# A conditioned state-space and gated-MLP block: column values in PSUM, the skip term's diagonal built on the chip, and a new order for the side jobs

## The chip, the cores and the metric

The kernel runs on one core of one Trainium2 chip. Its time is the device time in microseconds of one execution. Beside it stands one execution taken with the hardware profiler, from which the engines' instructions, their waits and the DMA transfers are read. Engines are named as the profile names them: PE (TensorE matmul), PEld (TensorE weight load), DVE (VectorE), ACT (ScalarE), POOL (GpSimd), SP (SyncE, which only starts transfers here).

## The reference

One sequence of 2048 rows and 640 channels goes through a layer with adaptive layer norms. All is float32.

```python
mod = (silu(c) @ w_mod).reshape(1, 6, 1, 640)          # sa, ca, ga, sb, cb, gb
h = layernorm(x) * (1 + ca) + sa
# state-space convolution, 192 complex modes for each of the 640 channels d
K[d, l] = Re(sum_n C[d, n] * exp(dt[d] * A[d, n] * l) * dt[d] * B[d, n])   # l = 0..2047
y = irfft(rfft(h, 4096) * rfft(K, 4096))[:2048] + h * Dskip
x = x + ga * y
h = layernorm(x) * (1 + cb) + sb
x = x + gb * (((h @ w_gate) * (h @ w_up)) @ w_down)    # 640 -> 1536 -> 640
```

## The kernel before

The 640 channels are five blocks db = 0..4 of 128. For each block the kernel of the convolution, K, is never exponentiated position by position. From **seeds** (a few powers for each mode) it builds tables of phases and of magnitudes, and takes products of matrices of them.

The program has four stretches. Up to about 26 us the seeds of block 0 are made. Then come 40 **steps** n = 0..39, eight for each block, each of 16 channels; step n is three thirds t = 3n, 3n+1, 3n+2. In a step POOL builds the phase table Ph (integers, so that a turn wraps by itself) and the magnitude tables EQ and EP as outer products (L817, `outer`); ACT takes absolute value and sine and cosine of Ph (its helper is L320, to which every ACT operation is put down; tiles tra and trb hold the result); DVE multiplies the two into QtA, PtA, PtB and QtB (L872, L878, L898); PE multiplies P by Q into the PSUM tile kg (L913 for the A half, kg_ma, and L928 for the B half, kg_mb). Every second step a kg tile is complete and goes through ACT into Kt and from there into the forward transform by matrices (L950, L974, L995), the product with the transformed input (L1036 to L1042, on DVE) and the inverse transform (L1055, L1110). Phase table Ph(n), EQ(n) and EP(n) each have two buffers; QtA, QtB and PtB have one, so DVE's QtA(n+1) waits for PE's kg_ma(n).

All other work is cut into **side jobs** that are slipped in between the thirds:

- w_mod is loaded a third at a time into t_tw and t_ti (1600 KB each, L451), which hold constants of the transform later; PE multiplies it by silu(c) into rows of PSUM (L458), and ACT copies the rows out (TVa, TVb).
- u_fold (L470 to L505) turns the three rows of the first half into columns (PE, L477), works out the gain and shift columns from them on DVE (L481 to L492) and spreads the shift over partitions (PE, L498, L499). The layer norm's gain is folded into the channel's scale dt2 and into the skip column dcol.
- the 16 tiles of x are loaded (`<-A_u`, L560), and DVE takes their statistics (L568); rstd (L371 to L378, called by row_stats for tiles 0 to 5 and then 6 to 15) turns them into 1/sigma and -mean/sigma; ACT normalises and the tiles are stored to DRAM as hm (L580).
- the seeds of blocks 1 to 4, in 14 segments each (L642 to L760, with parts on every engine), the second half of block 0's magnitude seeds (`e0`: ACT's exponentials of LP, RH and RL between two table loads), and the phase and magnitude seeds' doubling on POOL (L777, `tab_ph` and `tab_eq`).

A table of numbers, SCHED, sets where each job stands. A number v belongs to slot v // 1000: slots -101 to -86 lie in the set-up, slots 0 to 241 are the two calls due(2t) and due(2t+1) of each third t, and 287 is the last step; the remainder orders jobs within a slot. A second table, SLOT, gives for each ring of buffers (PSUM's three banks psfa, psfb, psfc, and TV, W, f16, gh, hf and others in SBUF) the letter that each request in turn takes.

The **skip term** h * Dskip enters K at l = 0. The tile dskt [128 x 160] is zero but for one row in each quarter of partitions, filled by transfers: four 1x8x4 pieces of Dskip for block 0 in the set-up (L1410); for the other blocks, whose Dskip is scaled by the gain, dcol goes to DRAM (dgd, L492) and comes back in four 1x32x4 pieces (L508, dskip). Every second step a matmul of 8 columns adds it to kg (L917).

After the steps the rest of the transform runs to 485 us, and then the gated MLP to the end, with matrices in high and low halves (L1160 splits them, L1196 and L1611 are the products).

## Time and profile before

| what | value |
|---|---|
| three runs | 995.63, 998.5, 999.91 us, median 998.5 |
| the profiled execution's own time | 990.33 us |
| its span | 988.6 us |
| its mean granted clock of TensorE | 0.958 |
| PE, DVE, ACT, POOL busy | 90%, 77%, 59%, 58% of the span |
| matmuls, DVE, ACT, POOL instructions | 11190, 1311, 1019, 424 |
| w_mod pieces, issue to landing | 7.4 us and 7.5 us (medians) |

A row of the timeline or of a group gives the start, the time that the engine was busy (for xN, N instructions together), engine, line, operation, output and inputs, shapes and, in brackets, how long the engine stood idle before it and what it waited for last. A row of windows gives, for one stretch of time, each engine's busy time and its instructions, the granted clock (PEclk, 1.00 is full) and the transfers' share.

### The profile page before, as it was taken

Reading aid. Unit: us, or ns where it says so; the run is one execution under the profiler, and the core shown is the slowest. Engines: PE = TensorE matmul, PEld = TensorE weight load, DVE = VectorE, ACT = ScalarE, POOL = GpSimd, SP = SyncE. Lnnn points to the kernel's source line nnn. Section 1 sums busy time; section 2 is a strip of 40 time slices with the busy share of each in tenths; the row PEclk is TensorE's granted clock in tenths of the full one; section 3 lists DMA queues with packets and bytes.
Section 4 is the critical chain, followed back from the end, with each engine's and each line's share of the span. In section 5 each row is a group of like instructions: output and inputs, shape, how many; then the busy total and the mean of one; then the engine's idle time right before and its main releaser. Section 6 shows DMA issues by size and latency. Waiting matters only on the chain.

```text
span 988.6 us, 26668 instructions
## 1 busy us (share of the span) xinstructions
PE 887.3 (90%) x11190; PEld 726.3 (73%) x11190; DVE 760.7 (77%) x1311; ACT 579.9 (59%) x1019; POOL 577.4 (58%) x424
## 2 busy tenths in 40 slices
PE   4854898999798699989988999999999999999998
PEld 3643656676575477677666888889998888889998
DVE  8798479887988977896899877787585977677452
ACT  5769999977888797974664322235464332224330
POOL 4987899799779989960145667641022454451000
PEclk9976899999989989999999999999999999999999
DMA  7665666443545553558733453445536222212241
GB/s 243 240 172 196 224 211 205 142 138 120 142 151 142 172 155 106 183 187 281 217 102 106 134 186 104 137 159 168 198 134 216 85 80 80 81 54 77 83 161 54
DMA packets 141961, 148.96 MB, mean 151 GB/s; under 512 B 8976, under 2 KB 120080, under 8 KB 140432
## 3 DMA queue, kind: packets, MB, share of 16 engines
q1 hardware_dynamic: 140688, 146.33, 46.9%
q8 instruction: 88, 1.44, 0.6%
q10 hardware_dynamic: 1152, 0.92, 0.3%
q14 instruction: 33, 0.27, 0.1%
HBM read 108.36 MB, written 38.86 MB: 149 GB/s over the span
## 4 chain that ended last, share of the span: by engine, by line
PE 58%; DVE 14%; ACT 13%; issue 6%; POOL 5%; DMA 2%; SPq 0%; DVEq 0%; ACTq 0%; POOLq 0%
PE pa L1196 26%; PE pa L1611 16%; ACT tra L320 2%; ACT trb L320 2%; PE psfb L995 2%; DVE QtA L872 2%; PE psfc L995 2%; PE psfb L1055 1%; PE kg L928 1%; POOL EQ L817 1%; PE psfa L1055 1%; PE kg L913 1%; PE psfc L1055 1%; PE psfb L950 1%; PE psfa L995 1%
## 5 line engine op out<-in xcount | busy, mean ns | idle before, releaser
L817 POOL TENSOR_TENSOR EQ<-LQ,RH 128x1536 f32<-128x1536 f32 x40 | 124.2, 3105 | 15.1 <-DVE QtB L872 14.9
L320 ACT ACTIVATE z<-pa 128x512 f32<-128x512 f32 x24 | 14.4, 599 | 167.1 <-PE pa L1196 120.5
L1160 DVE TENSOR_TENSOR wsgl<-wga,wsgh 128x640 fp32r<-128x640 f32 x72 | 68.1, 948 | 46.8 <-ACT wsgh L320 46.6
L320 ACT ACTIVATE wsgh<-wga 128x640 fp32r<-128x640 f32 x72 | 52.6, 732 | 72.0 <-PE pa L1611 48.6
L1560 POOL TENSOR_TENSOR z<-z,s 128x512 f32<-128x512 f32 x24 | 33.5, 1394 | 98.6 <-DVE s L1559 98.6
L1611 PE MATMUL pa<-wsgh,sh 128*128 128x384 f32 (+1 forms) x304 | 69.6, 310 | 0.0
L1611 PE MATMUL pa<-wsgh,sl 128*128 128x384 f32 (+1 forms) x304 | 69.2, 308 | 0.0
L1611 PE MATMUL pa<-wsgl,sh 128*128 128x384 f32 (+1 forms) x304 | 69.1, 309 | 0.0
L1172 POOL TENSOR_TENSOR tf<-wur,wgb 128x256 f32<-128x256 f32 x24 | 19.2, 801 | 80.7 <-DVE wtl L1160 54.7
L817 POOL TENSOR_TENSOR EP<-LP,RH 128x768 f32<-128x768 f32 x40 | 66.1, 1652 | 0.0
L817 POOL TENSOR_TENSOR Phb<-LH,DH 128x1536 int32<-128x1536 int32 x20 | 62.3, 3113 | 2.2 <-ACT tra L320 2.1
L817 POOL TENSOR_TENSOR Pha<-LH,DH 128x1536 int32<-128x1536 int32 (+1 forms) x21 | 62.4, 2972 | 1.8 <-ACT trb L320 1.4
L872 DVE TENSOR_TENSOR QtA<-tra,EQ 128x1024 f32<-128x1024 f32 x40 | 47.0, 1216 | 17.0 <-ACT tra L320 8.5
L1160 DVE TENSOR_TENSOR wtl<-tf,wth 128x256 fp32r<-128x256 f32 (+1 forms) x72 | 59.9, 858 | 0.0
L872 DVE TENSOR_TENSOR QtA<-trb,EQ 128x1024 f32<-128x1024 f32 x40 | 47.0, 1215 | 12.2 <-ACT trb L320 7.0
L928 PE MATMUL kg<-QtB,PtB 64*32 64x64 f32 x2560 | 47.0, 225 | 8.1 <-DVE QtB L872 8.0
L928 PEld LDWEIGHTS kg<-QtB,PtB 64*32 64x32 f32 x2560 | 40.3, 112 | 15.5 <-DVE QtB L872 9.0
L1558 DVE TENSOR_TENSOR s<-pa,s 128x512 f32<-128x512 f32 x24 | 16.6, 690 | 45.2 <-PE pa L1196 40.1
L1196 PE MATMUL pa<-sl,wth 128*128 128x512 f32 x144 | 45.2, 395 | 2.1 <-DVE sl L1160 2.1
L1611 PEld LDWEIGHTS pa<-wsgh,sl 128*128 128x128 f32 x304 | 46.6, 188 | 0.0
L1611 PEld LDWEIGHTS pa<-wsgh,sh 128*128 128x128 f32 x304 | 46.5, 188 | 0.0
L1611 PEld LDWEIGHTS pa<-wsgl,sh 128*128 128x128 f32 x304 | 46.5, 188 | 0.0
(602 smaller groups left out, 2926.9 us busy)
## 6 DMA issues: line engine op xcount, KB each, us to landing
wga<-wdg SPq DMA_DIRECT2D x24, 640.0 KB, 3.9
wga<-B_w_gate SPq DMA_DIRECT2D x12, 640.0 KB, 6.1
wgb<-B_w_gate SPq DMA_DIRECT2D x24, 320.0 KB, 3.4
wur<-B_w_up SPq DMA_DIRECT2D x24, 320.0 KB, 3.9
xb<-x2d SPq DMA_DIRECT2D x6, 1280.0 KB, 6.8
TVb<-WD SPq DMA_DIRECT2D x22, 256.0 KB, 3.4
t_tw<-w_mod SPq DMA_DIRECT2D x3, 1600.0 KB, 7.4
t_ti<-w_mod SPq DMA_DIRECT2D x3, 1600.0 KB, 7.5
```

Source lines behind the costliest of these rows:

```text
L320: return S.activation(o, i, f, **kw)
L817: G.tensor_tensor(o.rearrange("p x (h l) -> p x h l", l=8), lo.unsqueeze(2).to_broadcast([P, rows, nh, 8]), hi.rearrange("p h x -> p x h") ...
L872: return [lambda h=h: V.tensor_tensor(Qt[:, :, :, 32 * h : 32 * h + 32], tr[:, ::-1] if h else tr[:, :, :, ::-1], e[:, :, 32 * h : 32 * h ...
L928: PE.matmul(kg[j * 32 : j * 32 + 32, dd, :], PtB[lo : lo + 64, c, r, :], QtB[lo : lo + 64, c, r, :], start=False, stop=dd == 7 and c == 1, ...
L995: PE.matmul(r[c][par * 64 : par * 64 + 64, i, :], t_tw[:, k0 + k, c, :], src[:, k, :], start=True, stop=True, tile_position=(0, par * 64))
L1055: PE.matmul(r[par][:, i], w, v, start=c == 0, stop=c == 1, tile_position=(lo, 0))
L1160: V.tensor_tensor(lo, v, hi, op=OP.subtract)
L1172: G.tensor_tensor(t[:, 0:2], u[:, 0:2], g[:, 0:2], op=OP.subtract)
L1196: PE.matmul(ps, w[a][:, k], x[b][:, l], start=n == 0 and m == 0, stop=n == 2 and m == len(ks) - 1)
L1558: V.tensor_tensor(S67[i], ps, S6[i], op=OP.add)
L1560: G.tensor_tensor(ZT[i], ZT[i], S67[i], op=OP.add)
L1611: PE.matmul(ACC[tb][t][c], x[:, ts], w[:, cs], start=st, stop=f == NF - 1 and n == 2 and (c == 0 or t % 2 == 1))
```

## The change

Three things are edited together.

1. **Columns in PSUM.** rstd gets a second form, used by row_stats only, that keeps its two temporaries in a PSUM bank; rv and ry share a tile. In u_fold the temporaries (gp, ggp, dg) lie in the bank that holds the transposed rows. The temporaries of exp_acc become slices of shr. The new rstd has one DVE instruction more than the old one; the fold has two more.
2. **Skip term.** dskt, dgd and the nine transfers go. dsel [128 x 5 x 32] and jsel [128 x 4 x 32] are built on DVE from the identity matrix in the set-up; the fold multiplies blocks 1 to 4 of dsel by the scaled Dskip; the matmul takes jsel as weights and eight columns of dsel.
3. **Order.** Every number of SCHED up to slot 243 and most letters of SLOT are new; those of the last step (287) stay, as do the steps themselves.

```diff
-    ml=(-88998, -91999, -98999),
+    ml=(8000, 2001, -93999),
...
+    def rstd(mv, rs, nm, v, y, ps=None):
+
+        if ps is not None:
+            m = mv.shape[1]
+            v, t = ps[:, 0:m], ps[:, 32 : 32 + m]
+            V.tensor_scalar(v, mv[:, :, 1], EPS, None, op0=OP.add)
+            act(y, v, AF.Sqrt)
+            V.reciprocal(rs, y)
+            V.tensor_tensor(v, v, rs, op=OP.mult)
+            V.tensor_tensor(v, v, rs, op=OP.mult)
+            V.tensor_scalar(v, v, -0.5, 1.5, op0=OP.mult, op1=OP.add)
+            V.tensor_tensor(t, v, rs, op=OP.mult)
+            V.tensor_tensor(rs, v, rs, op=OP.mult)
+            V.scalar_tensor_tensor(nm, t, -1.0, mv[:, :, 0], op0=OP.mult, op1=OP.mult)
+            return
...
-        V.tensor_scalar(g1, p3[:, 1], 1.0, 2.0, op0=OP.add, op1=OP.mult)
+        gp, ggp = pc[:, 64 : 64 + NB], pc[:, 96 : 96 + NB]
+        V.tensor_scalar(gp, p3[:, 1], 1.0, 2.0, op0=OP.add, op1=OP.mult)
...
-        V.tensor_tensor(dcol[:, 1:], dcol[:, 1:], gg[:, 1:], op=OP.mult)
-        SY.dma_start(dgd[P:].rearrange("(b p) -> p b", p=P), dcol[:, 1:])
+        dg = pc[:, 128 : 128 + NB - 1]
+        V.tensor_tensor(dg, ggp[:, 1:], dcol[:, 1:], op=OP.mult)
+        V.tensor_tensor(dsel[:, 1:], dg.unsqueeze(2).to_broadcast([P, NB - 1, 32]), dsel[:, 1:], op=OP.mult)
...
-            need(0 if n < 8 else 4, "dsk")
-            PE.matmul(kg[:, :, 0], ident, dskt[:, n - 1 : n + 1, :].rearrange("p t l -> p (t l)"), start=False, stop=False)
+            need(0 if n < 8 else 1, "dsk")
+            PE.matmul(kg[:, :, 0], jsel.rearrange("p j r -> p (j r)"), dsel[:, n // 8, n % 8 * 4 - 4 : n % 8 * 4 + 4], start=False, stop=False)
...
-        rstd(mv1[:, s_, :], rs1[:, s_], nm1[:, s_], rv[:, s_], ry[:, s_])
+        rstd(mv1[:, s_, :], rs1[:, s_], nm1[:, s_], rv[:, s_], ry[:, s_], ps=ring(ps_f, [P, 512], "psf"))
...
+            i4 = ident.rearrange("p (t j l) -> p t j l", t=8, j=4)
+            V.tensor_reduce(dsel[:, 1].rearrange("p (t l) -> p t l", t=8), i4.rearrange("p t j l -> p t l j"), axis=AX.X, op=OP.add)
+            V.tensor_reduce(jsel[:, :, 0], i4.rearrange("p t j l -> p j t l"), axis=AX.XY, op=OP.add)
+            V.tensor_scalar(dsel[:, 0], dsel[:, 1], dcol[:, 0:1], None, op0=OP.mult)
+            V.tensor_copy(dsel[:, 2:], dsel[:, 1:2].to_broadcast([P, NB - 2, 32]))
```

PE's queue from the first row of mod to kg_mb(1). t_tw and t_ti hold w_mod, sil is silu(c); the pair of kg matmuls with the skip term's 8 columns is step 1. Before:

```order
L458 MATMUL psfb<-t_ti,sil 128x256 x5
L458 MATMUL psfc<-t_ti,sil 128x384 x5
L458 MATMUL psfa<-t_tw,sil 128x384 x5
L458 MATMUL psfc<-t_tw,sil 128x256 x5
L913 MATMUL kg<-QtA,PtAa 32x64 x32
L928 MATMUL kg<-QtB,PtB 32x64 x32
L477 MATMUL psfb<-ident,TVa 128x1 x5
L477 MATMUL psfb<-ident,TVb 128x1 x5
L477 MATMUL psfb<-ident,TVa 128x1 x3
L477 MATMUL psfb<-ident,TVb 128x1 x2
L913 MATMUL kg<-QtA,PtAb 32x64 x32
L917 MATMUL kg<-dskt,ident 128x8
```

The same piece of PE's queue after (line numbers of the changed kernel, 12 to 13 higher):

```order
L471 MATMUL psfa<-t_ti,sil 128x384 x5
L925 MATMUL kg<-QtA,PtAb 32x64 x32
L471 MATMUL psfc<-t_ti,sil 128x256 x5
L940 MATMUL kg<-QtB,PtB 32x64 x32
L471 MATMUL psfc<-t_tw,sil 128x256 x5
L471 MATMUL psfb<-t_tw,sil 128x384 x5
L925 MATMUL kg<-QtA,PtAa 32x64 x32
L929 MATMUL kg<-dsel,jsel 128x8
L940 MATMUL kg<-QtB,PtB 32x64 x32
L490 MATMUL psfc<-ident,TVa 128x1 x5
```

Steps 0 and 1 now stand between the rows of mod, and the fold's transposes (L477, now L490) have moved from ahead of step 1 to behind it.

DVE's queue at step 19, where block 3's first seed operations stood (L649 to L652, of which the first waits for ACT). Before:

```order
L872 TENSOR_TENSOR QtA<-tra,EQ_146 128x32x32 x2
L649 TENSOR_SCALAR psfa<-pta,dt 128x192
L650 TENSOR_SCALAR pta<-psfa 128x192
L651 TENSOR_TENSOR psfa<-psfa,pta 128x192
L652 TENSOR_SCALAR prm<-psfa 128x192
L878 TENSOR_TENSOR PtAb<-trb,EP_148 128x1024
L898 TENSOR_TENSOR PtB<-tra,EP_148 128x512
```

And after:

```order
L884 TENSOR_TENSOR QtA<-tra,EQ_145 128x32x32 x2
L890 TENSOR_TENSOR PtAa<-trb,EP_147 128x1024
L910 TENSOR_TENSOR PtB<-tra,EP_147 128x512
L884 TENSOR_TENSOR QtB<-tra,EQ_145 128x16x32 x2
L1048 TENSOR_TENSOR TVb<-psfc,ghb 128x512
```

The four seed operations have left step 19; they stand three steps earlier.

DVE's queue at steps 29 and 30 (QtA<-trb opens step 30) with two segments of block 4's seed: L717 to L722, and L747 and L748, the copies out of PSUM that POOL's doubling of LQ takes. Before:

```order
L898 TENSOR_TENSOR PtB<-tra,EP_148 128x512
L872 TENSOR_TENSOR QtB<-tra,EQ_146 128x16x32 x2
L717 SCALAR_TENSOR_TENSOR prm<-ptb,dt_100,psfc 128x192
L718 SCALAR_TENSOR_TENSOR psfc<-psfc,ptb 128x192
L719 RECIPROCAL psfc<-psfc 128x192
L720 SCALAR_TENSOR_TENSOR pta<-pta,psfc 128x192
L721 TENSOR_TENSOR psfc<-pta,psfc 128x192
L722 TENSOR_SCALAR pta<-psfc 128x192
L872 TENSOR_TENSOR QtA<-trb,EQ_145 128x32x32 x2
L878 TENSOR_TENSOR PtAa<-tra,EP_147 128x1024
L747 COPY RL<-psfc 128x96 x2
L748 TENSOR_SCALAR ptb<-psfc 128x192
```

And after:

```order
L729 SCALAR_TENSOR_TENSOR prm<-ptb,dt_100,psfa 128x192
L730 SCALAR_TENSOR_TENSOR psfa<-psfa,ptb 128x192
L731 RECIPROCAL psfa<-psfa 128x192
L732 SCALAR_TENSOR_TENSOR pta<-pta,psfa 128x192
L733 TENSOR_TENSOR psfa<-pta,psfa 128x192
L734 TENSOR_SCALAR pta<-psfa 128x192
L910 TENSOR_TENSOR PtB<-tra,EP_147 128x512
L884 TENSOR_TENSOR QtB<-tra,EQ_145 128x16x32 x2
L884 TENSOR_TENSOR QtA<-trb,EQ_144 128x32x32 x2
L759 COPY RL<-psfa 128x96 x2
L760 TENSOR_SCALAR ptb<-psfa 128x192
L890 TENSOR_TENSOR PtAb<-tra,EP_146 128x1024
```

The copies (now L759, L760) have moved ahead of PtA(30); the six operations L717 to L722 (now L729 to L734) have moved from behind QtB(29) to ahead of PtB(29). Elsewhere the order also changes in ways that move single jobs by a third or two: e0's exponentials from step 1 to directly behind the first copy of pta on ACT, with its pair of table loads shared (one load fewer there); rstd's two halves from slot 22 to slots 12 and 18, apart, so that they switch the sine table out and back twice instead of once; seven x tiles ahead of the first w_mod piece on SP instead of two; and block 3's L702 (now L714) ahead of QtA(22) instead of behind it.

243 lines of the change are left out of this document (118 added, 125 removed), and 34 rows, old and new, of tables (d, g, pre, q).

## The prediction

> **What bounds the kernel now.** The page first, then one row of windows for each stretch (length, then busy us of PE, PEld, DVE, ACT, POOL; granted clock; transfers).
>
> ```profile
> span 988.6 us, 26668 instructions
> PE 887.3 (90%) x11190; PEld 726.3 (73%) x11190; DVE 760.7 (77%) x1311; ACT 579.9 (59%) x1019; POOL 577.4 (58%) x424
> ```
>
> ```profile
> 26.00:71.00 45.00, 34.71 (x572) 27.31 (x572) 37.92 (x77) 33.48 (x61) 44.29 (x26) 0.85 0.67 203
> 71.00:110.00 39.00, 20.80 (x384) 16.47 (x388) 28.68 (x59) 37.29 (x57) 28.39 (x21) 0.65 0.55 191
> 110.00:250.00 140.00, 126.95 (x2854) 91.59 (x2850) 112.44 (x163) 123.75 (x211) 132.92 (x77) 0.96 0.54 169
> 250.00:285.00 35.00, 29.44 (x581) 22.39 (x582) 31.19 (x54) 32.73 (x56) 22.52 (x18) 0.85 0.54 159
> 485.00:988.60 503.60, 489.89 (x2590) 425.59 (x2584) 360.13 (x593) 189.08 (x365) 190.11 (x177) 0.99 0.37 120
> ```
>
> PE's 90% says nothing of the part that changes. From 485 us on PE is busy for 489.9 of 503.6 us and the change touches nothing there: a microsecond saved earlier moves this stretch forward whole, and nothing more can be won in it. In the steps another engine leads. POOL, with its outer products, is busy for 44.3 of 45 us to 71 us and for 132.9 of 140 us from 110 to 250 us. Between these lie two stretches in which POOL has time to spare and ACT has none: 37.3 of 39 us from 71 to 110, and 32.7 of 35 us from 250 to 285, where DVE is full as well (31.2). So I read next POOL's own timeline for its long stops:
>
> ```profile
> 75.73 3.10 POOL L817 TENSOR_TENSOR EQ<-LQ,RH 128x1536 f32<-128x1536 f32 x1 [4.97 <-DVE QtB L872]
> 184.31 3.11 POOL L817 TENSOR_TENSOR EQ<-LQ,RH 128x1536 f32<-128x1536 f32 x1 [4.82 <-DVE QtB L872]
> 278.76 0.39 POOL L753 TENSOR_TENSOR DL<-ptb 128x96 int32<-128x96 int32 x1 [8.01 <-issue]
> 358.10 0.36 POOL L811 COPY LQ<-RL 128x96 f32<-128x96 f32 x1 [2.88 <-DVE RL L747]
> ```
>
> Each stop is a place where DVE came too late: twice with QtB, which frees a buffer of EQ, and twice with a seed that POOL has to double. What the new order puts ahead of DVE's instruction at these four places decides the time. At 184 us I find the same instructions in the same order ahead of QtB; this stop stays.
>
> **The start (steps 0 to 3).** What DVE does ahead of QtB(3), whose end releases EQ(5) at 75.7 us:
>
> ```profile
> 21.92 0.89 DVE L568 BATCH_NORM_STATS2 st<-gha 128x6 f32<-128x320 f32 x2 [0.82 <-DMA gha<-A_u]
> 39.32 2.36 DVE L872 TENSOR_TENSOR QtA<-tra,EQ 128x1024 f32<-128x1024 f32 x2 [0.89 <-PE kg L913]
> 47.22 0.17 DVE L481 TENSOR_SCALAR mcol<-psfb 128x5 f32<-128x5 f32 x1 [2.26 <-PE psfb L477]
> 47.42 0.43 DVE L482 TENSOR_SCALAR mcol<-mcol 128x5 f32<-128x5 f32 x1
> 60.76 2.36 DVE L872 TENSOR_TENSOR QtA<-tra,EQ 128x1024 f32<-128x1024 f32 x2 [0.85 <-POOL LQ L777]
> 70.07 0.72 DVE L371 TENSOR_SCALAR rv<-mv 128x6 f32<-128x6 f32 x1
> 72.17 0.17 DVE L371 TENSOR_SCALAR rv<-mv 128x10 f32<-128x10 f32 x1
> ```
>
> Four waits, 0.82 + 0.89 + 2.26 + 0.85 = 4.8 us, stand on the way. The first falls to x tiles loaded earlier, the second to kg_ma(0) moved ahead of the rows of mod, the third to the fold moved behind step 1. Waits in a queue this full come back in part further down; I count half, 2.4 us. Against it DVE gets dsel and jsel, five operations in all; the nearest rows by size are 0.89/2 us for a reduction over 320 and 0.17 us for a copy of a few columns, so 0.5 to 2.2 us, of which I take 1.0.
>
> The columns in PSUM: the same operation on 6 or 10 columns took 0.72 us once and 0.17 us once, and L482 took 0.43 us. The excess, 0.55 and 0.26 us, shows while POOL is in a table. Over fold and row statistics I put it at 1.3 us in all (between nothing and 2), all of which goes. The Trainium skill, "SBUF — State Buffer", section "Who interferes with whom", says that a DVE operation with two inputs in SBUF, or in a two-port mode, and a GpSimd operation that reads SBUF exclude each other for a whole instruction. By that rule a single blocked column could wait for a whole table of 3.1 us and the gain would be several times mine; the rows above show an excess of 0.55 us at most, and I go by them.
>
> So DVE alone would bring QtB(3) forward by 2.4 + 1.3 - 1.0 = 2.7 us. The first stop is 4.97 us, and 5 us is the most that can be had there. Now ACT, which is full right behind it:
>
> ```profile
> 22.30 0.37 ACT L320 ACTIVATE TVb<-psfb 1x256 f32<-1x256 f32 x1 [4.90 <-PE psfb L458]
> 25.52 0.48 ACT L320 ACTIVATE TVa<-psfa 1x384 f32<-1x384 f32 x1 [2.85 <-PE psfa L458]
> 46.74 1.28 ACT L320 ACT_TABLE_LOAD   x1
> 50.26 0.42 ACT L320 ACTIVATE RL<-RL 128x288 f32<-128x288 f32 x1
> 265.10 1.28 ACT L320 ACT_TABLE_LOAD   x1
> 266.39 0.36 ACT L320 ACTIVATE ptb<-ptb 128x192 f32<-128x192 f32 x1
> 266.67 0.32 ACT L320 ACTIVATE psfa<-ptb 128x192 f32<-128x192 f32 x1
> ```
>
> e0's exponentials with their load run from 46.74 to 50.68 us, 3.9 us, and the load back takes another 1.3: 5.2 us leave the steps for the set-up, where ACT stood idle for 4.90 and 2.85 us. The second switch to the square root and back puts 2 x 1.28 = 2.6 us into the steps. ACT's chain is shorter by 2.6 us. DVE and ACT agree on about 2.6 us; I take **-2.5 us**, with bounds of 0 and -5.
>
> A load costs what its row says: the operation at 266.39 starts 1.29 us after the load at 265.10. The Trainium skill, "ScalarE: Activation LUTs", section "What ACT_TABLE_LOAD costs", gives about 1.28 us and another 1.38 us of draining for each switch. This rule speaks against the change, which has one load more in all (25 for 24): by it that load would cost 2.7 us in place of 1.3 and the whole sum would be -2.8 instead of -4.2. The row shows no such drain.
>
> **Step 19 and block 3's seed.**
>
> ```profile
> 238.38 0.42 DVE L649 TENSOR_SCALAR psfa<-pta,dt 128x192 f32<-128x192 f32 x1 [3.05 <-ACT gha L320]
> 239.38 0.69 ACT L320 ACTIVATE tra<-ab,halfpi 128x512 f32<-128x512 f32 x1
> 241.03 0.68 DVE L898 TENSOR_TENSOR PtB<-tra,EP 128x512 f32<-128x512 f32 x1
> 265.46 2.34 DVE L872 TENSOR_TENSOR QtA<-trb,EQ 128x1024 f32<-128x1024 f32 x2
> ```
>
> L649 and its three followers leave. DVE's 3.05 us of waiting do not all come back, since PtB(19) needs ACT's cosine, done at 239.38 + 0.69 = 240.07, and started at 241.03: 1.0 us is to be had, and I add 0.2 for the small ACT operation that goes with them: -1.2. Against it, three steps later, L702 stands ahead of QtA(22) and waits for ACT's root, which ends at 266.67 + 0.32 = 266.99 while QtA(22) began at 265.46: up to +1.5, less if ACT is early. Half of that, +0.7. Together **-0.5 us**, bounds -4 (the wait and part of the stop at 278 us) and +1.9.
>
> **Step 30 and block 4's seed.**
>
> ```profile
> 347.80 1.27 DVE L872 TENSOR_TENSOR QtB<-tra,EQ 128x512 f32<-128x512 f32 x2
> 350.51 3.10 POOL L817 TENSOR_TENSOR EQ<-LQ,RH 128x1536 f32<-128x1536 f32 x1
> 352.02 0.36 DVE L722 TENSOR_SCALAR pta<-psfc 128x192 f32<-128x192 f32 x1
> 356.44 1.23 DVE L878 TENSOR_TENSOR PtAa<-tra,EP 128x1024 f32<-128x1024 f32 x1
> 357.70 0.42 DVE L747 COPY RL<-psfc 128x96 f32<-128x96 f32 x2
> ```
>
> POOL's stop of 2.88 us ends with L747. Ahead of PtA it comes 1.23 us earlier, so **-1.2 us**. The price is QtB(29), now behind L717 to L722, six operations that follow it up to 352.02 + 0.36 = 352.38. It ended at 347.80 + 1.27 = 349.07, so they take 3.3 us, and EQ(31) started only at 350.51: 1.4 us of cover. What is over, 1.9 us, POOL loses ahead of a stop that is longer than that. Bounds +1.9 (no gain, the loss whole) and -2.9.
>
> **The skip term.**
>
> ```profile
> L917 PE MATMUL kg<-dskt,ident 128*128 128x8 f32 x40 | 8.2, 278 | 0.0
> ```
>
> The row's last field is PE's waiting ahead of it: none, so the nine transfers were hidden, and their going is worth nothing. On SP they make room, which the x tiles use. The new matmul has the same shape and count. Taken at 0, bounds -0.5 and +0.5.
>
> **Sum.** -2.5 - 0.5 - 1.2 = -4.2 us. The profiled execution took 990.33 us for its span of 988.6; it lies 8.2 us under the median of the runs, 998.5. I carry the difference over: 998.5 - 4.2 = **994.3 us**. About 0.5%, 5 us, is what a measurement of this kernel can tell from no change.
>
> **The rivals.**
>
> *More is won.* The first stop vanishes whole (-5), L649's wait comes through at the next stop too (-2), and the stop at 358 us goes (-2.9): -9.9, with ACT giving back 1: about 989.5 us. For it: all three are waits on DVE, and each loses its cause. Against: ACT's 37.3 of 39 us and 32.7 of 35 us leave it no room.
>
> *Nothing is won.* What the start saves is spent at the stop of 184 us (unchanged) and in the ACT-bound stretch from 250 us, and the extra load takes the rest: about 998 us. For it: a stretch that another engine fills takes up an earlier start of POOL's. Against: stops end with DVE, which starts earlier itself.
>
> *Slower.* The w_mod pieces come too late, and PE stands in front of step 1 with them.
>
> ```profile
> 18.59 3.67 PE L458 MATMUL psfb<-t_tw,sil 128*128 128x256 f32 x10
> 22.10 3.39 PE L458 MATMUL psfa<-t_tw,sil 128*128 128x384 f32 x10
> 32.51 3.46 PE L458 MATMUL psfa<-t_tw,sil 128*128 128x384 f32 x10 [0.43 <-DMA t_tw<-w_mod]
> 47.11 1.94 PE L913 MATMUL kg<-QtA,PtAb 128*32 128x64 f32 x64
> t_tw<-w_mod SPq DMA_DIRECT2D x3, 1600.0 KB, 7.4
> ```
>
> Seven x tiles now lie ahead of the first piece, five more than before: 5 x 320 KB are the bytes of one piece, 7.4 us. In the worst case PE's first rows start at 18.59 + 7.4 = 26.0 and end at 33.1. Only then is t_tw free for the third piece, which lands 7.4 us later, at 40.5, and whose two rows (3.46 and about 2.3 us) end at 46.2: still ahead of 47.11, where step 1's kg_ma started. If that piece also shares the transfers with the second one, another 7.4 us, the rows end at 53.6, kg_ma(1) and QtA(2) behind it come 6.5 us later than before, and the start's term is +6.5 in place of -2.5: with the other terms +4.8, 1003.3 us, and up to 1007 with the bounds. The point from which it decides is kg_ma(1) starting after 47 us. For it: before, PE already waited 0.43 us for this piece. Against: the dskt transfers ahead are gone, and x tiles are small.
>
> **How the numbers follow.** The forecast 0.40; it lies close to the edge of what can be told, so half of it is faster and half the same. More is won 0.23 (faster). Nothing is won 0.15 (same). Slower 0.22, of which 0.05 stays within 0.5%. Faster 0.20 + 0.23 = 0.43, same 0.20 + 0.15 + 0.05 = 0.40, slower 0.17. The range runs from 985, just below all lower bounds together (-5 - 4 - 2.9 - 0.5 = -12.4, 986.1), to 1004, which takes in the greater part of the last rival. The forecast's own range, half-way from it to its bounds on each side, is 990 to 998.
>
> **What would show it.** Right, if in the changed profile POOL's stop ahead of EQ(5) is 2 to 3 us instead of 4.97, DVE's wait ahead of the fold is gone, no DVE operation of 5 to 10 columns takes over 0.3 us, block 3's first seed operation waits less than 1 us, POOL waits about 1.7 us ahead of LQ at step 30, ACT has 25 table loads, and the MLP begins about 4 us earlier. Wrong, if PE waits for t_tw ahead of step 1 or the MLP begins later than at 486 us.

## The result, and the profile after

The changed kernel is slower. Twenty runs of it have a median of 1000.9 us (995.45 to 1007.82), twenty of the kernel before beside them 995.38 us (991.16 to 999.91): a ratio of 1.0055, 95% interval [1.0037, 1.0074]. Twelve more runs, made later beside the experiments, gave 997.5 us and 1.0020 [0.9998, 1.0041], where 1.004 to 1.007 was expected; by themselves they cannot be told from no change. So the loss is about 5 us by the first set and 2 by the second. The 32 runs together have a median of 1000.4 us.

The profiled execution took 1001.23 us with a span of 999.4 us. First the head of the page after:

```profile
span 999.4 us, 26670 instructions
PE 894.6 (90%) x11190; PEld 728.3 (73%) x11190; DVE 760.6 (76%) x1319; ACT 581.7 (58%) x1020; POOL 577.5 (58%) x424
```

Every engine has the same work as before to within 2 us, but for PE, which is busy for 7 us more with as many matmuls. So the difference lies in waiting and in PE's speed. The windows after follow, over the same four stretches and from the last d to the end. By the last d the start of the last addition into a staging tile xs is meant (L1122, in the kernel before L1110), near the end of the transform; six more additions of this kind, into xb and Kt, come behind it.

```profile
26.00:71.00 45.00, 36.39 (x612) 28.68 (x615) 42.10 (x98) 37.17 (x61) 44.53 (x26) 0.79 0.69 233
71.00:110.00 39.00, 25.84 (x521) 18.12 (x516) 27.26 (x47) 37.74 (x60) 32.47 (x24) 0.94 0.63 208
110.00:250.00 140.00, 120.40 (x2698) 87.98 (x2687) 107.08 (x156) 114.44 (x194) 128.25 (x75) 0.95 0.49 148
250.00:285.00 35.00, 28.03 (x496) 19.09 (x486) 28.97 (x53) 30.23 (x51) 19.36 (x16) 0.85 0.32 86
492.62:999.40 506.78, 491.30 (x2592) 426.25 (x2588) 360.73 (x594) 189.40 (x365) 189.94 (x177) 0.99 0.37 120
```

The last of these stretches before:

```profile
484.52:988.60 504.08, 490.37 (x2592) 425.73 (x2588) 360.61 (x594) 189.08 (x365) 190.11 (x177) 0.99 0.37 120
```

From 26 to 110 us the engines do more than before: DVE has 42.1 us of work in the first 45 us where it had 37.9, and 98 instructions where it had 77. From 110 us on POOL does less in the same time (128.3 for 132.9 us, then 19.4 for 22.5). And the stretch from the last d to the end, which the prediction took to be fixed, has grown from 504.08 to 506.78 us.

POOL's long stops after:

```profile
69.89 3.11 POOL L829 TENSOR_TENSOR EQ<-LQ,RH 128x1536 f32<-128x1536 f32 x1
...
179.54 3.11 POOL L829 TENSOR_TENSOR Pha<-LH,DH 128x1536 int32<-128x1536 int32 x1 [7.61 <-ACT tra L320]
183.88 3.11 POOL L829 TENSOR_TENSOR EQ<-LQ,RH 128x1536 f32<-128x1536 f32 x1 [1.22 <-DVE QtB L884]
...
281.04 0.36 POOL L823 COPY LQ<-RL 128x96 f32<-128x96 f32 x1 [9.58 <-DVE RL L759]
...
358.08 3.10 POOL L829 TENSOR_TENSOR EQ<-LQ,RH 128x1536 f32<-128x1536 f32 x1 [4.55 <-DVE QtB L884]
...
365.49 0.36 POOL L823 COPY LQ<-RL 128x96 f32<-128x96 f32 x1 [2.71 <-DVE RL L759]
```

EQ(5) comes at 69.89 in place of 75.73 us, without a stop. At 184 us the lead is gone: EQ(15) starts at 183.88, before at 184.31. Its stop has shrunk from 4.82 to 1.22 us, but a new one of 7.61 stands just ahead of it, released by ACT. The stop for block 3's seed has grown from 8.01 to 9.58 us, and EQ(31), which before had no stop and started at 350.51, now waits 4.55 us and starts at 358.08.

DVE in the start: the first row of the fold, and one row of each half of the row statistics:

```profile
45.44 0.17 DVE L374 TENSOR_SCALAR psfa<-mv 128x6 f32<-128x6 f32 x1
...
50.86 0.17 DVE L495 TENSOR_SCALAR psfc<-psfc 128x5 f32<-128x5 f32 x1 [0.43 <-PE psfc L490]
...
58.41 0.17 DVE L374 TENSOR_SCALAR psfc<-mv 128x10 f32<-128x10 f32 x1
```

The fold's wait is 0.43 us for 2.26, and the small column operations take 0.15 to 0.21 us where single ones took 0.72 and 0.43. Two rows of PE answer the rival that saw w_mod come late:

```profile
28.86 3.49 PE L471 MATMUL psfa<-t_ti,sil 128*128 128x384 f32 x10 [0.95 <-ACT TVa L320]
...
39.82 3.49 PE L471 MATMUL psfb<-t_tw,sil 128*128 128x384 f32 x10 [0.50 <-ACT TVb L320]
```

PE waits for ACT's copies of earlier rows, not for w_mod, and step 1's kg_ma starts at 43.24 us (before 47.11).

### The profile page after: what moved, and what is told of

The parts are those of the page before. It is cut to its first block, busy times and chain, and to the rows that moved or that the text cites. A ratio compares the mean times of both kernels' runs of the same rounds, so it can differ in the third digit from the quotient of the medians.

```text
span 999.4 us, 26670 instructions
## 1 busy us (share of the span) xinstructions
PE 894.6 (90%) x11190; PEld 728.3 (73%) x11190; DVE 760.6 (76%) x1319; ACT 581.7 (58%) x1020; POOL 577.5 (58%) x424
## 4 chain that ended last, share of the span: by engine, by line
PE 64%; ACT 10%; DVE 9%; POOL 7%; issue 5%; DMA 3%; SPq 0%; DVEq 0%; ACTq 0%; POOLq 0%
PE pa L1208 26%; PE pa L1624 16%; PE psfc L1007 2%; PE kg L925 2%; PE kg L940 2%; PE psfa L1007 2%; PE psfb L1007 2%; POOL EQ L829 2%; PE psfa L986 1%; PE psfa L1067 1%; DVE QtA L884 1%; ACT trb L320 1%; ACT tra L320 1%; POOL Phb L829 1%; POOL LH L789 1%
## 5 line engine op out<-in xcount | busy, mean ns | idle before, releaser
L829 POOL TENSOR_TENSOR Pha<-LH,DH 128x1536 int32<-128x1536 int32 x20 | 62.2, 3112 | 12.1 <-ACT tra L320 12.1
L829 POOL TENSOR_TENSOR Phb<-LH,DH 128x1536 int32<-128x1536 int32 (+1 forms) x21 | 62.4, 2972 | 3.5 <-ACT trb L320 3.0
```

The lines of the kernel that those rows point to most:

```text
L829: G.tensor_tensor(o.rearrange("p x (h l) -> p x h l", l=8), lo.unsqueeze(2).to_broadcast([P, rows, nh, 8]), hi.rearrange("p h x -> p x h") ...
```

## The experiments

All ratios are to the kernel before, timed beside it on the same chip, with 12 runs of the kernel unless another number is given. In most of them whole stretches of the two orders were put together: each entry of SCHED takes its old or its new value according to the slot, and the letters of SLOT are carried over so that each buffer follows from the one ahead. EQ(n) is the start of POOL's EQ table of step n, given as a difference to the first profile of the kernel before.

**The code edits on the old order**, in two forms:

```diff
-    SCHED, SLOT of the changed kernel
+    SCHED, SLOT of the kernel before
-        rstd(mv1[:, s_, :], rs1[:, s_], nm1[:, s_], rv[:, s_], ry[:, s_], ps=ring(ps_f, [P, 512], "psf"))
+        rstd(mv1[:, s_, :], rs1[:, s_], nm1[:, s_], rv[:, s_], ry[:, s_])                                  # e1_code
+        rstd(mv1[:, s_, :], rs1[:, s_], nm1[:, s_], mcol.rearrange("p a b -> p (a b)")[:, s_], ry[:, s_])  # e7_code
```

Fold and skip term are the changed ones; the row statistics stay in SBUF. In e1_code their two temporaries share memory, which spoils the normalised values, so that this kernel serves for its time and its order alone; in e7_code they lie apart.

> The old order of all side jobs, with the skip term built on the chip and the fold's columns in PSUM (the row statistics stay in SBUF, since no bank is free where the old order has them). Theory (the two code edits are neutral, the order does it): POOL's EQ(39) within 1 us of 430.4 us, its value in the profile of before, and a time within 2 us of before's. Rival (the code edits themselves cost, for instance dsel on DVE or PSUM traffic): EQ(5) later than 75.7 us, and 4 to 6 us slower than before.

> As the run e1_code (old order, skip term on the chip, fold's columns in PSUM), but with the row statistics' two temporaries in places of their own, where that run let them overlap. Theory (the code edits cost nothing): time 0 to 4 us under before's, EQ(39) at 430 to 433.5 us. Rival (that run's time hung on its values): 997 us or more.

992.93 us, 0.9969 [0.9946, 0.9992], and 991.25 us, 0.9965 [0.9944, 0.9987]. The code does not cost time; it saves some 3 us. What is lost is lost by the order. In the profiles EQ(39) stands at +2.67 us in e1_code, where 1 us was expected, and at +0.17 in e7_code.

**The new order up to a slot, the old one from there.** One entry shows how the values change hands:

```diff
 c of block 0, piece 0: new (105002, 105004, 108001, 109000), old (103000, 105000, 108003, 108004)
 c of block 1, piece 0: new (139001, 139004, 143000, 144000), old (138001, 140001, 141002, 145001)
 c of block 3, piece 1: new (220000, 222000, 226000, 229002), old (218001, 222000, 227000, 228001)
 e2_front    new in slots to 85, old from 86
 e3_to120    new in slots to 120, old from 121
 e6_old217   new in slots to 216, old from 217
```

> The changed kernel's code and its new order up to slot 85 (steps 0 to 14), then the old order, with the letters of the rings renamed so that they fit. Theory (the start's gain is real, but from step 9 on DVE, ACT and PE set the pace and eat it): EQ(5) at about 70 us, 5 to 6 us ahead of before; EQ(15) only 0.5 to 2 us ahead; EQ(39) 0 to 2 us ahead, at 428.5 to 430.4 us; time 0 to 2 us under before's. Rival 1 (the new start delays later transfers and is itself the loss): EQ(39) at 435 us or later, 4 us slower or more. Rival 2 (POOL sets the pace all through, so the start's gain lasts): EQ(39) at 424 to 425 us, 5 us faster.

> The changed kernel's code and its new order up to slot 120 (steps 0 to 19), then the old order. Theory (what is lost is lost in three places of the new order behind step 20): EQ(15) at 183.9 us as in the changed kernel, EQ(39) at 429.5 to 430.5 us, time within 2 us of before's. Rival (the loss has its cause ahead of step 20 and only shows later): EQ(39) at 436 us or later and 5 us slower than before.

> The changed kernel with the old order from slot 217 on (steps 36 to 39 and the end of the transform). Theory (the new order of these last slots costs a part of its own): EQ(39) at 437 to 438.5 us as in the changed kernel, but from the last L1122 to the MLP's first matmul 23 us as before instead of 25.8, time 2 to 4 us under the changed kernel's. Rival (the end is longer because everything ahead of it came late): 25 to 26 us stay, time within 1 us of the changed kernel's.

| kernel | median us | ratio and interval |
|---|---|---|
| e7_code, old order | 991.25 | 0.9965 [0.9944, 0.9987] |
| e2_front, new to slot 85 | 990.7 | 0.9940 [0.9905, 0.9974] |
| e3_to120, new to slot 120 | 991.44 | 0.9953 [0.9923, 0.9983] |
| e6_old217, new to slot 216 | 995.71 | 1.0007 [0.9984, 1.0029] |
| the changed kernel, new throughout | 1000.9 | 1.0055 [1.0037, 1.0074] |

A staircase: the new start is worth about 2.5 us at the end of the program (inside the intervals of e2_front and e7_code), slots 121 to 216 (steps 20 to 35) cost about 5 us, and what lies behind slot 217 about 5 more by the first twenty runs of the changed kernel, about 1 by the twelve later ones. e2_front beats both kernels; it was expected 0 to 2 us under the kernel before and came out 5 under. Its profile does not show this lead: EQ(39) stands at +1.35 us there, beside a first profile of the kernel before that was a lucky one (below).

**The late order alone, and the middle alone.** e4_late is the kernel before, code and order, with the new order from slot 121; t_mid is the changed kernel with the old order in slots 121 to 216.

```diff
 e4_late     code of before; old in slots to 120, new from 121
 t_mid       changed code;   new in slots to 120, old in 121 to 216, new from 217
```

> The kernel before with its own code and order up to slot 120, then the new order. Theory (the new order behind step 20 is the loss): EQ(22), EQ(24), EQ(31) fall back as in the changed kernel (by about 1.7, 1.9 and 4.6 us), EQ(39) at 437 to 438.5 us, time 6 to 8 us over before's. Rival (the loss has its cause ahead of step 20, or in the code edits): EQ(39) within 1.5 us of 430.4 us, time within 2 us of before's.

> The changed kernel with the old order in slots 121 to 216 (thirds of steps 20 to 35) and the new order ahead of and behind them, with the new last banks. Theory (the middle's loss of some 5 us, at the seed operations ahead of QtA(22) and at c(2,2,2) ahead of kg_ma(29), is its own and adds to that of the end): EQ(24) and EQ(31) no more than 1 us behind EQ(20) by the difference to the kernel before, last d to first matmul 25 to 26 us, ratio 0.997 to 1.001. Rival (an end in the new order costs 5 us whatever stands ahead, or takes back what the middle saves): ratio 1.002 to 1.006.

e4_late: 1005.85 us (9 runs), 1.0083 [1.0056, 1.0110]; on the old start the late order costs 8 us. t_mid: 996.46 us, 1.0002 [0.9977, 1.0027]. In its profile EQ(20), EQ(24) and EQ(31) stand at +4.52, +3.77 and +3.76 us: nothing is lost between steps 20 and 31 with the old order there. The losses of the middle (e6_old217 beside e3_to120) and of the end (t_mid beside e3_to120), about 5 us each, add up to that of the first twenty runs.

**Step 29, repaired.** The matmuls of c(2,2,2) (the inverse transform of a piece of block 2, L1067) go behind kg_mb(29), and block 4's L729 to L734 behind QtB(29):

```diff
-    c(2,2,2): (165000, 167001, 178006, 182004)
+    c(2,2,2): (165000, 167001, 182000, 182004)
-    q of block 4, segments 10 and 11: 178004, 182000
+    q of block 4, segments 10 and 11: 180000, 182001
```

> The changed kernel with two jobs put back at steps 29 and 30: the matmuls of L1067 (one quarter's inverse transform of block 2) behind kg_mb(29) instead of ahead of kg_ma(29), and block 4's L729 to L734 behind QtB(29) instead of ahead of PtB(29). Theory (these two moves are the loss at step 31): DVE's wait ahead of QtA(30), 4.44 us in the changed kernel, falls under 1 us, POOL's EQ(31) starts 3 us behind before instead of 7.6, EQ(39) at 433 to 435 us instead of 438.0, time 3 to 5 us under the changed kernel's. Rival (block 4's seed is late for other reasons, and POOL waits for it whatever stands at step 29): POOL waits longer ahead of LQ at step 30 instead, EQ(39) at 437 us or later, time within 1 us of the changed kernel's.

The profile of the changed kernel at this place, PE first, then DVE:

```profile
356.08 0.79 PE L1067 MATMUL psfc<-TVa,t_ti 64*128 64x128 f32 x2 [1.36 <-ACT ghc L320]
...
360.27 1.93 PE L925 MATMUL kg<-QtA,PtAa 128*32 128x64 f32 x64
```

```profile
356.65 1.28 DVE L884 TENSOR_TENSOR QtB<-tra,EQ 128x512 f32<-128x512 f32 x2
362.37 2.35 DVE L884 TENSOR_TENSOR QtA<-trb,EQ 128x1024 f32<-128x1024 f32 x2 [4.44 <-PE kg L925]
365.10 0.42 DVE L759 COPY RL<-psfa 128x96 f32<-128x96 f32 x2 [0.37 <-PE psfa L641]
```

PE has L1067 in front of kg_ma(29), and L1067 waits for ACT. So kg_ma(29) ends late, and QtA(30), which overwrites what it reads, waits 4.44 us; L759 behind it, for which POOL stops ahead of LQ, comes late with it. EQ(31) is another matter: it is released by QtB(29), which stands ahead of QtA(30) and behind the six operations L729 to L734. With the repair, PE and then POOL:

```profile
356.18 1.94 PE L925 MATMUL kg<-QtA,PtAa 128*32 128x64 f32 x64
358.57 1.17 PE L940 MATMUL kg<-QtB,PtB 64*32 64x64 f32 x64
359.67 0.37 PE L1067 MATMUL psfc<-TVa,t_ti 64*128 64x128 f32 x1
```

```profile
357.19 3.11 POOL L829 TENSOR_TENSOR EQ<-LQ,RH 128x1536 f32<-128x1536 f32 x1
```

POOL's stop ahead of EQ(31) is gone, and the difference does not grow from EQ(30) to EQ(31) (+6.69, +6.68; the changed kernel +3.00, +7.57). Which of the two moves does it, the other profiles tell: from QtB(28) to QtB(29) all seven with the six operations ahead of PtB(29) lose 3.4 us against the kernel before, the nine others, which have them behind QtB(29) or in the old place, nothing (-0.07 to -0.01). But in this execution 4.5 us were lost between EQ(21) and EQ(22), and the time, 1000.42 us, 1.0057 [1.0027, 1.0087], is that of the changed kernel. The cause of the loss at EQ(31) is shown; that its repair pays by itself is not.

**Step 22, repaired.** One DVE operation (L714, block 3's seed) goes back behind QtA(22):

```diff
-    q of block 3, segment 8: 132002
+    q of block 3, segment 8: 133000
```

> The changed kernel with one DVE operation, L714 of block 3's seed, put back behind QtA(22). Theory (it waits 1.9 us for ACT ahead of QtA(22) and holds POOL's tables up): EQ(24) starts no more than 0.5 us later than EQ(22) does by the difference to the kernel before, in place of 1.9 us; the time falls by 1 to 2 us, too little to tell from the changed kernel's. Rival (another stop, at POOL's doubling of LQ, gives the same delay): EQ(24) still loses 1.5 to 2 us.

DVE ahead of QtA(22) in the changed kernel, then in the repaired one:

```profile
268.50 0.36 DVE L714 TENSOR_SCALAR psfa<-ptb 128x192 f32<-128x192 f32 x1 [1.90 <-ACT psfa L320]
```

```profile
267.44 2.36 DVE L884 TENSOR_TENSOR QtA<-trb,EQ 128x1024 f32<-128x1024 f32 x2 [0.31 <-ACT Wa L320]
```

And POOL's stop in the repaired one, 9.58 us in the changed kernel:

```profile
279.75 0.35 POOL L823 COPY LQ<-RL 128x96 f32<-128x96 f32 x1 [7.77 <-DVE RL L759]
```

From EQ(22) to EQ(24) the difference grows by 0.07 us for 1.86 in the changed kernel. In this execution, as in e5_step29, 4.5 us had been lost just ahead, between EQ(21) and EQ(22); but so they had in the changed kernel's second profile (below), and that one loses 1.92 us from EQ(22) to EQ(24) all the same. The time, 997.63 us, 1.0026 [0.9999, 1.0052], cannot be told from the changed kernel's beside it (997.5 us, 1.0020), where a fall of 1 to 2 us, too small to tell, was expected.

**The tail: banks, buffers, and both.** Behind the last step the order of the instructions is nearly the old one, but SLOT's letters are not. From the last d to L1284 the kernel before takes 23.04 us and the changed one 25.78. (L1284 is the transpose with which the MLP's main part begins; the expectations call it the first matmul of the MLP, but the first products with w_gate, L1338, run ahead of it.) Three kernels take this apart: the old PSUM banks in the changed kernel, the new PSUM banks on the old order (with e7_code's edits), and the old buffers hf (the normalised tiles) in the changed kernel.

```diff
 SLOT psf from slot 240 on                          # l_letters
-    babcabdbcfecdafbcfaebadcabfaecdaebebadbae
+    baacbaeacdfbedcabdcbeafedecbdcfaebfceadbf
 SLOT psf, the last 39 of e7_code                   # t_banks
-    cabcecafdbefacbfabecdefeabfadcebdaecfbd
+    bacbfbadeafcdbadcebcfacbdceafcebebcfbce
 SLOT hf, the last 14                               # t_hf
-    bbacacbacacbcc
+    baabacbacbacba
```

> The changed kernel, every instruction in the order it has there; only the banks that the last requests for PSUM take (from slot 240 on) are the ones of the kernel before. Theory (the banks' turns make the tail longer, since a transpose waits for the copy that frees its bank): the stretch from the last d to the first matmul of the MLP falls from 25.8 us to about 23, EQ(39) stays 7 to 8 us behind, and the time is 2 to 4 us under the changed kernel's, about 997 to 999 where the kernel before stands at 995.4. Rival (the tail is longer because the engines reach it in another state, not because of banks): that stretch stays above 25 us and the time stays at 1.005 to 1.006 of the kernel before.

> The code edits on the old order (as e7_code, which took 0.9965 of the kernel before), with nothing else changed than the PSUM banks taken from slot 240 on, which are now the changed kernel's. Theory (the banks' turns cost 2.0 to 2.7 us by themselves): last d to first matmul of the MLP 25 to 26 us instead of 23.0, end of that d to the end of the span 506.5 to 507.5 us instead of 503.8, time 993 to 995, ratio 0.998 to 1.0005. Rival (the banks cost only behind the new order): 23 us, ratio 0.9965 as before.

> The changed kernel with the buffers of the normalised tiles (hf) from slot 240 on as in the kernel before and everything else, the new PSUM banks too, unchanged. Theory (only bank and buffer together hold ACT up: its fifth pair of normalisations no longer needs the fourth group of transposes): DVE's wait for ACT ahead of the third L1323 falls from 2.4 us to under 1, the third matmul of L1338 starts 13.2 to 13.7 us after the last d in place of 15.5, PE's granted clock stays at 1.00 there, last d to first matmul of the MLP 22.5 to 23.2 us, and the time is 2 to 3 us below the changed kernel's. Rival (the bank alone holds PE up, 1.75 us): third L1338 at 15 us or later, 25 us or more.

| kernel | last d to L1284 us | last d to end us | median us | ratio and interval |
|---|---|---|---|---|
| kernel before | 23.04 | 504.08 | 995.38 | |
| changed kernel | 25.78 | 506.78 | 1000.9 | 1.0055 [1.0037, 1.0074] |
| l_letters, old banks | 22.91 | 504.75 | 998.03 | 1.0012 [0.9981, 1.0044] |
| t_hf, old hf buffers | 22.54 | 504.23 | 997.23 | 1.0017 [0.9990, 1.0043] |
| t_banks, new banks on the old order | 22.55 | 503.87 | 993.93 | 0.9988 [0.9969, 1.0008] |

The ratio of l_letters is to be held beside that of the later runs of the changed kernel (997.5 us, 1.0020), with which it was timed: of the 2 to 4 us that were expected nothing shows on the clock.

The theory of the first of these experiments, that the banks alone make the tail longer, fell with t_banks, which has the new banks and no longer tail. The rows show why. In the changed kernel PE transposes the normalised tiles (L1317), ACT and DVE make the high and the low half (L1323, L1325), and PE multiplies (L1338). PE:

```profile
504.28 0.66 PE L1317 MATMUL psfb<-ident,hfc 128*128 128x128 f32 x4 [1.75 <-DVE a L1323]
...
508.08 0.80 PE L1338 MATMUL psg<-hl,wsgh 128*128 128x512 f32 x1 [2.67 <-DVE hl L1325]
508.67 0.63 PE L1338 MATMUL psg<-hh,wsgh 128*128 128x512 f32 x1
```

ACT, then DVE, of the same kernel:

```profile
505.04 0.88 ACT L320 ACTIVATE hfc<-xb,hr,hr 128x128 f32<-128x128 f32 x2 [1.71 <-PE psfb L1317]
```

```profile
506.62 0.81 DVE L1323 TENSOR_SCALAR a<-psfa,colT 128x512 f32<-128x512 f32 x1 [2.39 <-ACT hh L320]
```

The fourth group of transposes takes bank psfb once more and waits 1.75 us for DVE's copy out of it. ACT's fifth pair of normalisations writes hfc, the buffer that this same group reads, so it waits too (1.71), and with it the copies hh behind it on ACT; DVE waits for those (2.39), and PE for DVE (2.67). In t_hf the bank is the same but the fifth pair has another buffer. PE, ACT and DVE of t_hf:

```profile
507.84 0.65 PE L1317 MATMUL psfb<-ident,hfb 128*128 128x128 f32 x4 [1.36 <-DVE a L1323]
...
509.82 0.50 PE L1338 MATMUL psg<-hl,wsgh 128*128 128x512 f32 x1 [0.85 <-DVE hl L1325]
510.16 0.39 PE L1338 MATMUL psg<-hh,wsgh 128*128 128x512 f32 x1
```

```profile
506.79 0.87 ACT L320 ACTIVATE hfa<-xb,hr,hr 128x128 f32<-128x128 f32 x2
```

```profile
508.36 0.81 DVE L1323 TENSOR_SCALAR a<-psfa,colT 128x512 f32<-128x512 f32 x1 [0.57 <-ACT hh L320]
```

PE still waits for the bank, 1.36 us, but ACT runs on, and the third matmul of L1338 starts 13.25 us after the last d in place of 15.46. In l_letters it is the bank that turns, and the buffer stays:

```profile
494.59 0.66 PE L1317 MATMUL psfa<-ident,hfc 128*128 128x128 f32 x4
...
498.38 0.50 PE L1338 MATMUL psg<-hl,wsgh 128*128 128x512 f32 x1 [2.67 <-DVE hl L1325]
```

Here the fourth group does not wait and that matmul starts 13.63 us after the last d. So either ring may repeat; only both together close the circle. A second part of the price is PE's clock: behind its wait the changed kernel's L1338 take 0.63 us each, with a granted clock of 0.50 from 508.6 to 512.6 us; in t_hf they take 0.39 at 1.00. In six profiled kernels with the new order, banks and buffers there (the changed one twice, l_p24, t_mid, e4_late, e5_step29) eight to ten of these matmuls were slow; in the first profiles of the kernel before and of e7_code five, in e1_code seven, in the others none. The wait alone does not do it: l_letters has the same 2.67 us ahead of L1338 and no slow matmul behind it. The changed kernel's PE had stood 1.75 us shortly before as well; what brings the clock down there was not tried. The six profiles with the circle have 506.3 to 507.4 us from the last d to the end, all eleven others 503.8 to 504.8. In the timed runs a gain of 2 or 3 us lies inside the intervals.

**Three places at once.** L714, step 29 and the old banks together:

> The changed kernel with three repairs: L714 behind QtA(22); c(2,2,2)'s matmuls behind kg_mb(29) and L729 to L734 behind QtB(29); the old banks from slot 240 on. Theory (these three places hold the loss): EQ(39) 3 to 4 us behind the first profile of the kernel before instead of 7.6, last d to first matmul of the MLP 23 us, time 993 to 996.5, ratio 0.998 to 1.001. Rival (the loss is spread over the order, and each repair only moves it on): EQ(39) still 6 us or more behind, ratio above 1.003.

994.24 us, 0.9969 [0.9945, 0.9993], beside 997.5 us and 1.0020 [0.9998, 1.0041] for the changed kernel at the same time; the ratio of the two means is 0.9962, interval [0.9936, 0.9989]. The repairs together win 3 to 4 us on the clock. In the trace not all went as expected: EQ(24) and EQ(31) keep their places (+1.68, +2.01), the stretch from the last d to L1284 is 22.91 us, but between EQ(32) and EQ(34) 2.5 us are lost that the changed kernel does not lose there, and EQ(39) is 5.77 us behind where 3 to 4 were expected.

**Both kernels once more.** The kernel before and the changed one, unchanged, with a new profile each:

> The kernel before, once more, for a second profile of it. Theory (its first profile was a lucky one around step 11, since two other runs with the same order there fell back 2.5 to 3.3 us): EQ(15) at 186.5 to 187.5 us instead of 184.3, EQ(39) at 432 to 434 us. Rival (those two runs differ for a reason of their own): EQ(15) at 184 to 185 us.

> The changed kernel once more, unchanged, beside the three others on the same chip. Every theory: ratio 1.004 to 1.007, EQ(5) 5.5 to 6 us ahead of the kernel before's first profile, last d to first matmul of the MLP 25 to 26 us. It tells how far EQ(15), EQ(24) and EQ(31) vary between two profiles of the same program: if EQ(31) lies within 1.5 us of the first profile's 358.1, a single profile can carry the differences between orders; if it does not, only the timed runs can.

The second profile of the kernel before has a span of 997.5 us where the first had 988.6: EQ(5) starts 5.47 us later, EQ(11) 9.16 us. The first profile, from which the prediction was made, was a lucky one. Most of the 5.47 us can be seen in the fold. Its eleven column operations (L481 to L491) take 6.35 us from the first to the last in this execution, 2.60 in the first profile and 2.89 in e4_late; their twelve successors in PSUM (L495 to L507) take 2.05 to 2.08 us in all fourteen profiles. The longest one, DVE and then POOL of the second profile:

```profile
53.43 3.06 DVE L491 TENSOR_TENSOR dcol<-dcol,mcol 128x4 f32<-128x4 f32 x1
```

```profile
53.38 3.09 POOL L817 TENSOR_TENSOR EQ<-LQ,RH 128x1536 f32<-128x1536 f32 x1
```

L491 has four columns and took 0.15 us in the first profile. Here it lasts as long as the table that POOL builds beside it, and ends 0.02 us behind it.

The second profile of the changed kernel has a span of 1000.8 us; EQ(31) lies at 356.5 us, 1.6 us from the first profile's 358.1, so a single profile does not carry differences of this size between orders. The table below goes by medians of all 17 profiles for that reason.

## Why the prediction was wrong

Three steps of it failed. The lead of the start was carried whole to the end, and half of it is gone at EQ(15). The moves at steps 19, 22 and 30 were counted as a gain of 1.7 us in all, and the stretch that holds them, EQ(15) to EQ(39), loses 5.2. The tail was put at nothing, and it costs 2.6.

Each row of the table has the medians over the profiled kernels with the old and with the new order in the greater part of that stretch (those with a repair in it counted as new):

| stretch, difference to the first profile of before, us | old order | new order | new less old |
|---|---|---|---|
| to EQ(5) | +0.47 (6 kernels) | -5.95 (11) | -6.42 |
| to EQ(15) | +2.68 (6) | -0.43 (11) | -3.11 |
| EQ(15) to EQ(30) | -0.22 (8) | +3.37 (9) | +3.59 |
| EQ(30) to EQ(39) | +0.06 (8) | +1.70 (9) | +1.64 |
| EQ(39) to the last d | +0.04 (8) | +0.72 (9) | +0.68 |
| last d to the end, without and with the circle | +0.11 (11) | +2.71 (6) | +2.60 |

The last five rows add up to +5.40 us. The medians of the two kernels differ by 5.5 us in the first set of runs and by 2.1 in the second, so the sum agrees with the first set alone.

**The start, -2.5 us.** The mechanism was right and its size too small: at EQ(5) the lead was 5.84 us in the first profile and 6.4 by medians, more than the lower bound of -5, since the set-up too was 0.8 us quicker. The step that failed was counting half of DVE's four waits: of the four only the fold's is left, with 0.43 us for 2.26, and DVE's idle time up to the end of QtB(3) fell from 11.9 to 5.7 us.

The columns were sized by one execution, and that was the second mistake here: its rows show an excess of 0.55 us at most, but L491 in the second profile of the kernel before has one of 2.9 us. The Trainium skill, "SBUF — State Buffer", section "Who interferes with whom", lets a blocked column wait for a whole GpSimd instruction. The traces agree with it, since L491 ends 0.02 us behind POOL's table, and the two columns that the prediction read end 0.03 us behind the POOL instruction beside them (70.79 for 70.76, 47.85 for 47.82): 0.55 us was what happened to be left of it.

**"This stop stays" (184 us), and "a microsecond saved earlier moves the last stretch forward whole".** The second sentence failed first: half of the lead is gone at EQ(15). By medians of the same kernels DVE's QtB(7) leads by 8.8 us, QtB(12) by 3.2 and EQ(15) by 3.1, so it is lost in steps 8 to 12, ahead of the stop. Two rows of DVE there, QtA(8) and PtB(12):

```profile
119.06 2.35 DVE L884 TENSOR_TENSOR QtA<-trb,EQ 128x1024 f32<-128x1024 f32 x2 [5.59 <-PE kg L925]
...
163.42 0.69 DVE L910 TENSOR_TENSOR PtB<-trb,EP 128x512 f32<-128x512 f32 x1 [2.51 <-ACT trb L320]
```

QtA(8) waits for kg_ma(7), and PE has a matmul of the transform in front of kg_ma(7) (L986, which itself waits 2.03 us for POOL), as it has L1067 in front of kg_ma(29). How much of the lead goes in these steps differs between executions: in the first profile 0.9 us is left at QtB(12), in the second 4.1. DVE's instructions at the stop were the same, as said; ACT's were not. The changed kernel's ACT switches tables ahead of the sine of step 13, and POOL waits 7.61 us for that sine:

```profile
168.81 1.28 ACT L320 ACT_TABLE_LOAD   x1
...
177.50 1.28 ACT L320 ACT_TABLE_LOAD   x1
178.79 0.60 ACT L320 ACTIVATE tra<-Pha 128x512 f32<-128x512 int32 x1
```

This new stop only uses up the lead that POOL's tables still had: EQ(15) waits last for QtB(13), ahead of which DVE does not stand still from 170.7 us on, and from QtB(12) to EQ(15) the lead shrinks by no more than 1.2 us in any of the eleven profiles. Past the start the prediction had followed DVE and POOL only; in steps 8 to 12 DVE waits for PE and ACT.

The load itself cost what was said. The sine starts 1.29 us after the load at 177.50. The Trainium skill, "ScalarE: Activation LUTs", section "What ACT_TABLE_LOAD costs", adds 1.38 us of draining for a switch; this trace shows none.

**Step 19 and block 3's seed, -0.5 us, bounds -4 and +1.9.** DVE after the change:

```profile
238.67 1.28 DVE L884 TENSOR_TENSOR QtB<-tra,EQ 128x512 f32<-128x512 f32 x2
243.71 0.69 DVE L1048 TENSOR_TENSOR TVb<-psfc,ghb 128x512 f32<-128x512 f32 x1 [3.76 <-ACT PtAb L320]
```

QtB(19) does come earlier, as forecast: 238.67 us here. Then DVE stands 3.76 us at L1048, a product of the transform that takes what PE makes (its L1007 runs to 243.8 us). (The row names ACT's PtAb, which by the profile ended last, but at 243.46 us; PE's ends are modelled.) A new wait has taken the place of the removed one, one row further down, and I had not followed DVE past QtB: from QtB(18) to QtB(20) the eight profiles with the new order on both sides of step 20 lose 1.7 to 4.7 us. At QtA(22) the price was put at half of 1.5 us; the row has 1.90 us, and l_p24 shows that this one operation makes the loss from EQ(22) to EQ(24). From EQ(15) to EQ(30) the stretch costs 3.6 us, above the upper bound.

**Step 30 and block 4's seed, -1.2 us, bounds -2.9 and +1.9.** The price of the six operations was right: 3.4 us in all seven profiles, for 3.3. The cover of 1.4 us was not, since it supposes that DVE is no later than POOL. In the first profile QtB(28) stands at +5.49 us and EQ(30) at +3.00, so EQ(31) lost 4.57 us and not 1.9; in the seven profiles it loses 2.1 to 5.0. The gain did not come either: POOL's stop ahead of LQ hardly changed (2.71 us for 2.88), because L759 stands behind QtA(30), and QtA(30) waits for a kg_ma(29) that has L1067 in front of it. The order of PE at this place was not read. By medians 1.7 us are lost up to EQ(39).

**The tail, no term at all, +2.7 us.** I had it that the change touches nothing there, because the steps and the entries of the last slot stay. The letters of SLOT do not. This is the second largest piece of the loss, and no bound held it.

**The skip term, 0.** That the nine transfers were hidden agrees with L929, which has PE waiting for nothing:

```profile
L929 PE MATMUL kg<-dsel,jsel 128*128 128x8 f32 x40 | 8.5, 286 | 0.0
```

But the code edits on the old order are 3 us faster, more than the terms for the columns (-1.3), for dsel and jsel (+1.0) and for the skip term (0, bounds -0.5 and +0.5) allow. The profiles of e7_code and of the kernel before differ by less than 0.3 us at EQ(5), EQ(30) and EQ(39); but the latter was a lucky one. Beside the second profile of the kernel before, the fold of e7_code is 4.3 us shorter. So the likely place of the 3 us is the columns, worth -1.3 in one execution and several times as much in another; that they make the whole difference of the medians is not shown.

**The base, 998.5 us.** The median of the three runs shown is 3 us above that of the twenty. A sum of -4.2 on 995.4 would have been 991.2 us.

**The rivals.** "Slower" was right in its sign and wrong in its mechanism: w_mod was in time (a piece takes 9.2 us from issue to landing for 7.4, yet kg_ma(1) starts at 43.24 us, ahead of the deciding 47). So it is luck that the range, which was stretched to 1004 us for w_mod, takes in the measured time. "More is won" holds as far as EQ(5). "Nothing is won" had the outcome of the first half, a start whose gain is spent on the way, but not the place: the stop at 184 us is not where it goes.

## What to carry to other kernels

A wait that is taken away is a gain only if the next row of the same engine, and of the engine that hands it its data, is ready: follow the lead engine by engine to the next place at which all four queues meet, before counting anything at the end. When a table of buffer letters changes, the order of instructions tells nothing; ask of every buffer that is taken twice in a row who must let it go, and whether the two rings close a circle. And an order tuned piece by piece can be taken apart piece by piece: the new start with the old rest (e2_front, 990.7 us, 0.9940 [0.9905, 0.9974]) beats both kernels, though the code edits on the old order alone (e7_code, 991.25 us, 0.9965) cannot be told from it. A wait that one profile shows is sized for that execution only; a second profile of the same kernel costs little and here would have moved the columns' term from 1.3 us to over 4.

## What the runs showed of the hardware

The granted clock at the same place of the same program differs from execution to execution. The changed kernel, t_mid and t_hf have the same program up to slot 120. From 110 to 125 us, in this order:

```profile
110.00:125.00 15.00, 12.97 (x266) 10.10 (x259) 8.54 (x12) 12.02 (x21) 15.00 (x8) 0.89 0.50 147
```

```profile
110.00:125.00 15.00, 12.74 (x201) 9.21 (x191) 7.10 (x10) 10.67 (x18) 14.80 (x8) 0.70 0.45 132
```

```profile
110.00:125.00 15.00, 12.75 (x206) 9.25 (x197) 7.13 (x10) 10.73 (x18) 14.83 (x8) 0.70 0.47 139
```

At a clock of 0.89 PE does 266 matmuls in these 15 us, at 0.70 only 201 and 206 in the same busy time. Up to QtB(7) the three are within 0.1 us of each other; EQ(11) stands at -4.46 us in the first and at -0.35 and +0.53 in the others, EQ(15) at -0.43, +4.68 and +5.67. That the clock makes this difference is argued from these rows, not tried. It fits the scatter of the runs: twenty of one kernel reach over 9 to 12 us.
